# Attention on quarters of the TensorE array: state's part of y four heads at a time, scores 64 keys wide without the masked quarter

## The chip, the cores and the metric

The kernel runs on one core of a Trainium2 chip. The core has a matrix engine (TensorE, PE in the rows; its weight loads are PEld), a vector engine (VectorE, DVE), an activation engine (ScalarE, ACT), GpSimd (POOL) and a sync engine (SyncE, SP) on whose queue all DMAs of this kernel are issued. The metric is the device time of one execution in microseconds (us), as the median of several runs; lower is better.

## The reference

Three layers follow each other: a linear attention with a decaying state, a layer with `h * cos(h)`, and a gated layer. Only the first is touched by the change.

```python
def _attn_ref(q, k, v):                      # (4, 8, 768, 64): batch, heads, tokens, head size
    gamma = 1.0 - 2.0 ** (-5.0 - np.arange(H))
    scale = 1.0 / np.sqrt(D)
    for t in range(S):
        state = gamma * state + outer(k[:, :, t], v[:, :, t])
        y[:, :, t] = scale * (q[:, :, t] @ state)
    return y

def reference(...):
    x = attn_out as (3072 tokens, 512 features)
    h = x @ w_in                              # 512 x 2048
    x = (h * cos(h)) @ w_out                  # 2048 x 512
    return (silu(x @ w_gate) * (x @ w_val)) @ w2_out   # 512 x 1536, 1536 x 512
```

## The kernel before

**Attention in chunks.** Time is cut into chunks of 128 tokens (`C`) of one batch, 24 chunks in all (`NCH`; chunk `c` belongs to batch `c % 4`). A chunk has four steps. *Scores* (`scores_pe`, L306): for each of the 8 heads, a 128x128 matrix of keys against queries, in two PSUM banks `sc` (even heads in one, odd heads in the other). *Decay* (`scores_decay`, L321): DVE multiplies each bank with a table `cst` that holds the decay and zeros where the key comes after the query; the result is `s` in SBUF. *Values* (`values_pe`, L330): `y` of the chunk in one PSUM bank, first the part that comes from the state (L337, not for the first four chunks), on which the part of the chunk itself is accumulated (L344). *State* (`state_pe`, L358; `state_add`, L373): `u`, the keys against the values, is added to the state and the state is decayed, on DVE and POOL. `y` is then split into a high and a low part (`split_hi` on ACT, L113; `split_lo` on DVE, L116), which are the columns of `x` for the next layer.

The heads lie in pairs: q and k have feature rows (64 rows for the even head of a pair, 64 for the odd one), so a matmul of scores uses 64 of the 128 rows of the array, one of state's part 64 rows and 64 columns, the other matmuls of attention 128 rows and 64 columns. These matmuls are in full float32; the trace has two records for each. The large matmuls (`h` L418, `o` L501) are 128x128x512.

**The order of the work.** From the first chunks on, attention is mixed into the middle layer. This runs in 96 units: unit n makes a tile `h` (12 matmuls, L418), sends it through ACT and DVE, and PE then does the output matmuls `o` (12, L501) of the unit two before. `attn_at` (L806) lists which steps of attention stand at the end of which unit's code: chunks 4 to 7 in units 1 to 7 (with the states of 0 to 3 in unit 0), chunks 8 to 11 in units 22 to 29, and chunks 12 to 23 in units 32 to 79, four units to a chunk: scores, decay, values, state. Work for DVE and ACT that a step leaves behind (`late_mid`, `late_act`, `late_x`) runs within the next unit. In the same units ACT, DVE and POOL prepare weights (`Weight`, L121).

**Buffers.** The PSUM pool `ps_a` has two banks, tag "a": scores take both, y one, u one. `qpool` has three buffers that q and k of a chunk (`load_qk`), and k and v by token (`load_kv`), take in turn; a load waits on SP's queue until the buffer's last reader is done. `load_qk(c + 1)` stands with the scores of chunk c, `load_kv(c + 1)` with its values. Raw weights of the first layer use the places of the first eight chunks' q, k and v.

Of the kernel before, what the change touches and what calls it, by code (L numbers as in the profile page):

```python
# [20 lines left out]
DM = H * D  # L21
# [36 lines left out]
NCONST = 1548  # L58


def constants():
    gamma = 1.0 - 2.0 ** (-5.0 - np.arange(H, dtype=np.float64))
    i = np.arange(C, dtype=np.float64)
    t = np.zeros((P, NCONST), np.float64)
    head = 2 * np.arange(NP)[None, :] + (np.arange(P)[:, None] // D)
    t[:, CQ:CQ + 512] = (gamma[head][:, :, None] ** (i + 1.0) / math.sqrt(D)).reshape(P, 512)
    back = i[None, :] - i[:, None]
    by_half = gamma.reshape(NP, 2).T[None, :, :, None]
    decay = np.where(back >= 0, 1.0, 0.0)[:, None, None, :] * by_half ** np.maximum(back, 0.0)[:, None, None, :]
    t[:, CDEC:CDEC + 1024] = (decay / math.sqrt(D)).reshape(P, 1024)  # L70
    t[:, CV:CV + H] = gamma[None, :] ** -(i[:, None] + 1.0)
    t[:, CG:CG + NP] = gamma[head] ** float(C)
    return t.astype(np.float32)

# [2 lines left out]
def fused(ctx: ExitStack, tc: tile.TileContext, qkv, w1, w2, consts, out):  # L77
# [34 lines left out]
    def split_hi(src, dst):  # L112
        nc.scalar.activation(out=dst[:, 0], in_=src, func=AF.Copy)  # L113
# [156 lines left out]
    def load_qk(c, pool=qpool, tag="qkv"):  # L270
        if c >= NCH:
            return
        if pool is wpool:
            both = wpool.tile([P, 4, 512], F32, tag=tag, name="qkv")
            qkv_t[c] = [both[:, 0:2], both[:, 2:4]]
        else:
            qkv_t[c] = [pool.tile([P, 2, 512], F32, tag=tag, name="qk")]
        nc.sync.dma_start(out=qkv_t[c][0].rearrange("p a b -> p (a b)"), in_=qkv[c, :, 0:1024])

    def load_kv(c, part=slice(0, 2)):  # L280
        if c >= NCH:
            return
        if len(qkv_t[c]) == 1:
            qkv_t[c].append(qpool.tile([P, 2, 512], F32, tag="qkv", name="kv"))
# [35 lines left out]

    def scores_decay(c, half, place=None):  # L321
        if half == 0:
            p, t = place or (spool, "s")
            s_t[c] = p.tile([P, 2, 4, C], F32, tag=t, name="s")
        nc.vector.tensor_tensor(
            out=s_t[c][:, half], in0=ps_t.pop((c, half)),
            in1=cst[:, CDEC + 512 * half:CDEC + 512 * half + 512].rearrange("p (a b) -> p a b", a=4), op=ALU.mult,
        )

    def values_pe(c, place=(ps_a, "a")):  # L330
        qk, kv = qkv_t[c]
        first = c < B
        y = place[0].tile([P, NP, C], F32, tag=place[1], name="y")
        if not first:
            for h in range(H):
                r = slice(D * (h % 2), D * (h % 2) + D)
                nc.tensor.matmul(  # L337
                    out=y[r, h // 2, :], lhsT=states[c % B][r, h // 2, :],
                    rhs=qk[r, 0, (h // 2) * C:(h // 2 + 1) * C],
                    start=h < 2, stop=False, skip_group_check=True,  # L340
                )
        for h in range(H):
            r0 = D * (h % 2)
            nc.tensor.matmul(  # L344
                out=y[r0:r0 + D, h // 2, :],
                lhsT=kv[:, 1, h * D:(h + 1) * D],
                rhs=s_t[c][:, h % 2, h // 2, :],
                start=first and h < 2, stop=h >= H - 2, skip_group_check=True,
            )
        ps_t[c, "y"] = y  # L350

    def values_x(c):
        j, o = c // CPB, (c % CPB) * C
        if o == 0:
            x_t[j] = xpool.tile([P, 2, KD, T], F32R, tag=f"x{(j + (j > 1)) % 2}", name="x")
        return ps_t.pop((c, "y")), x_t[j][:, :, :, o:o + C]

    def state_pe(c, place=(ps_a, "a")):  # L358
        if c // B == NCB - 1:
# [25 lines left out]
    def attn_scores(c, place=None, load=True):  # L385
        if load:
            load_qk(c + 1)
        scores_pe(c)
        scale_queries(c)
        scale_keys(c)  # L390
        late_mid.append(lambda: scores_decay(c, 0, place))

    def attn_decay(c):
        late_mid.append(lambda: scores_decay(c, 1))

    def attn_values(c, place=(ps_a, "a"), load=True):
        values_pe(c, place)
        if load:
            load_kv(c + 1)
        y, x = values_x(c)  # L400
        late_act.append(lambda: split_hi(y, x))
        late_x.append(lambda: split_lo(y, x))
# [301 lines left out]
    def second_layer():  # L704
# [97 lines left out]
    n6 = len(units)  # L802


    o2 = (ps_o, "o2")
    attn_at = {  # L806
        0: [(attn_state, 0), (attn_state, 1), (attn_state, 2, o2), (attn_state, 3, (ps_o, "o3"))],
        1: [(attn_scores, CPB + 1, None, False), (attn_decay, CPB + 1), (attn_values, CPB, o2, False)],
        2: [(attn_values, CPB + 1, (ps_a, "a"), False)],
        3: [(attn_scores, CPB + 2, None, False), (attn_decay, CPB + 2)],  # L810
        4: [(attn_values, CPB + 2, (ps_a, "a"), False), (attn_state, CPB)],
        5: [(attn_scores, CPB + 3, None, False), (attn_decay, CPB + 3)],
        6: [(attn_values, CPB + 3, (ps_a, "a"), False), (attn_state, CPB + 1)],
        7: [(attn_state, CPB + 2), (attn_state, CPB + 3)],
    }
    for i in range(2 * CPB):
        c = 2 * CPB + i // 2
        attn_at[HEAD + M1 - 1 + i] = [(step, c) for step in four_steps[2 * (i % 2):2 * (i % 2) + 2]]
# [38 lines left out]
    with tc.manual_schedule():  # L857
        warm = tmp.tile([P, T], F32, tag="r", name="warm")
        nc.vector.memset(warm, 0.0)
        wz = warm.bitcast(mybir.dt.bfloat16)  # L860
        idle = ps_h.tile([P, T], F32, tag="h", name="idle")

# [43 lines left out]

        def first_decay(c):
            for half in range(2):
                scores_decay(c, half, (wpool, "w11") if c % 2 else None)

        def first_hi(c):
            first_x[c] = values_x(c)
            split_hi(*first_x[c])

        first_x = {}
        steps = {
            "sc": first_scores, "m": first_decay, "y": values_pe, "xh": first_hi,
            "xl": lambda c: split_lo(*first_x[c]), "k": scale_keys, "q": scale_queries,
        }
        for a in (  # L920
            "sc0 m0 y0 sc1 xh0 xl0 m1 size0 y1 xh1 xl1 low0 round0 sc2 m2 y2 merge0 xh2 sc3 m3 hi0 xl2 lo0 "
# [24 lines left out]
        for n, (kind, j, m, first, last) in enumerate(units):  # L946
            if n == n5:
                run(late_act)
                run(late_x)
                run(late_mid)  # L950
                attn.close()
                w2pool.append(ctx.enter_context(tc.tile_pool(name="w2pool", bufs=1)))
                for i in range(2):
                    Place(w2pool[0], f"v{i}").give()
                Twin("x1")
            if HEAD + 1 <= n < M1 + 1:
                fetch_w1(n - 1)
            elif n == M1 + 1:
                load_qk(2 * CPB)
                load_kv(2 * CPB)  # L960
            a, b = take(halves_at.get(n, 0)) if n < FIRST2 else take2(n)
            hidden1(j, m, first, a, b, n == 0)
            if n == FIRST2 or jobs2.get(n, "x")[0] == "b":
                fetch_w2()
            for step, *args in x_at.get(n, []):
                step(*args)
            pending.append((kind, j, m, first, last))
            steps = attn_at.get(n, [])
            if n == HEAD - 1:
                for step, *args in steps:  # L970
                    step(*args)
                steps = []
            while len(pending) > SKEW:
                output_unit(*pending.pop(0))
            for step, *args in steps:
                step(*args)
# [58 lines left out]
```

## Time and profile before

| | |
|---|---|
| median of 3 runs | 1191.59 us (1190.84 to 1195.01) |
| the profiled execution | 1192.35 us |
| its span, first to last instruction | 1190.6 us |
| PE busy | 1168.4 us, 98% of the span |
| PEld busy | 952.1 us |
| DVE, ACT, POOL busy | 644.4, 588.4, 105.4 us |
| granted clock of TensorE, mean | 0.996 of full speed |

Matmuls are pipelined and overlap in the rows, so the time that a group of matmuls costs is read from where the next group starts, not from its busy time. Attention and the middle layer fill the span up to about 648 us; after that the gated layer runs, which the change does not touch.

### The profile page before, as it was taken

Reading aid. Unit: us, or ns where it says so; the run is one execution under the profiler, and the core shown is the slowest. Engines: PE = TensorE matmul, PEld = TensorE weight load, DVE = VectorE, ACT = ScalarE, POOL = GpSimd, SP = SyncE. Lnnn points to the kernel's source line nnn. Section 1 sums busy time; section 2 is a strip of 40 time slices with the busy share of each in tenths; the row PEclk is TensorE's granted clock in tenths of the full one; section 3 lists DMA queues with packets and bytes.
Section 4 is the critical chain, followed back from the end, with each engine's and each line's share of the span. In section 5 each row is a group of like instructions: output and inputs, shape, how many; then the busy total and the mean of one; then the engine's idle time right before and its main releaser. Section 6 shows DMA issues by size and latency. Waiting matters only on the chain.

```text
span 1190.6 us, 15278 instructions
## 1 busy us (share of the span) xinstructions
PE 1168.4 (98%) x6096; PEld 952.1 (80%) x6096; DVE 644.4 (54%) x953; ACT 588.4 (49%) x847; POOL 105.4 (9%) x98
## 2 busy tenths in 40 slices
PE   7899999999999999999999999999999999999998
PEld 5688878887887878888888888878888888888877
DVE  4866764346566656666656555574444474444430
ACT  4958973346666666676855334342233342232220
POOL 2621211111211111110000000000000000000000
PEclk9999999999999999999999999999999999999999
DMA  9407833224886698588676646666448566546451
GB/s 363 194 4 276 321 125 108 97 98 181 318 323 234 232 343 320 170 310 316 250 274 240 245 160 240 246 229 248 195 164 322 208 241 266 194 157 267 169 238 36
DMA packets 54215, 265.51 MB, mean 223 GB/s; under 512 B 5760, under 2 KB 6016, under 8 KB 33152
## 3 DMA queue, kind: packets, MB, share of 16 engines
q1 hardware_dynamic: 54144, 264.53, 59.5%
q8 instruction: 48, 0.79, 0.3%
q14 instruction: 23, 0.19, 0.0%
HBM read 213.13 MB, written 51.38 MB: 222 GB/s over the span
## 4 chain that ended last, share of the span: by engine, by line
PE 89%; ACT 5%; DVE 2%; issue 2%; DMA 1%; POOL 1%; SPq 0%; DVEq 0%; POOLq 0%
PE h L418 20%; PE o L501 19%; PE o L688 16%; PE X L637 16%; PE Z L637 8%; PE Y L637 4%; ACT rw L146 2%; PE sc L314 2%; PE y L344 2%; PE y L337 2%; DMA rw<-in_w_dram 1%; PE u L365 1%; ACT f L130 1%; ACT w L113 1%; ACT g L481 0%
## 5 line engine op out<-in xcount | busy, mean ns | idle before, releaser
L688 PE MATMUL o<-wo,g 128*128 128x512 f32 x864 | 207.6, 392 | 1.4 <-ACT g L668 1.4
L418 PE MATMUL h<-x,w 128*128 128x512 f32 x780 | 193.0, 396 | 2.0 <-ACT w L113 1.7
L688 PEld LDWEIGHTS o<-wo,g 128*128 128x128 f32 x864 | 163.1, 189 | 36.4 <-ACT g L668 1.9
L501 PE MATMUL o<-g,w 128*128 128x512 f32 x780 | 187.7, 389 | 1.1 <-DVE x L116 1.1
L418 PEld LDWEIGHTS h<-x,w 128*128 128x128 f32 x780 | 144.1, 188 | 36.0 <-ACT w L113 2.5
L501 PEld LDWEIGHTS o<-g,w 128*128 128x128 f32 x780 | 146.2, 188 | 31.9 <-issue 1.5
L637 PE MATMUL X<-xo,wh 128*128 128x512 f32 x576 | 144.5, 389 | 0.0
L637 PEld LDWEIGHTS X<-xo,wh 128*128 128x128 f32 x576 | 108.0, 188 | 22.8 <-DVE xo L603 0.4
L668 ACT ACTIVATE g<-silu 128x512 fp32r<-128x512 f32 x72 | 45.5, 633 | 155.0 <-DVE silu L667 155.0
L461 ACT ACTIVATE n<-h 128x512 int32<-128x512 f32 x96 | 57.0, 594 | 92.8 <-PE h L418 92.4
L418 PE MATMUL h<-x,back 128*128 128x512 f32 x372 | 91.4, 394 | 0.0
L501 PE MATMUL o<-g,back 128*128 128x512 f32 x372 | 89.3, 389 | 0.0
L146 ACT ACTIVATE rw<-rw,above 128x1024 uint16<-128x1024 uint32 x34 | 89.0, 2618 | 0.1
L778 DVE TENSOR_TENSOR u<-Z,u 128x512 f32<-128x512 f32 x36 | 24.9, 691 | 116.5 <-PE Z L637 116.5
L501 PEld LDWEIGHTS o<-g,back 128*128 128x128 f32 x372 | 69.8, 188 | 14.5
L418 PEld LDWEIGHTS h<-x,back 128*128 128x128 f32 x372 | 68.7, 188 | 15.8 <-issue 1.2
L637 PE MATMUL Z<-xo,wh 128*128 128x512 f32 x288 | 73.2, 389 | 0.0
L637 PE MATMUL X<-x,wh 128*128 128x512 f32 x288 | 73.1, 389 | 0.0
L671 DVE TENSOR_TENSOR g<-silu,g 128x512 fp32r<-128x512 f32 x72 | 49.8, 692 | 36.0 <-ACT g L668 34.3
L131 POOL TENSOR_SCALAR f<-f 128x1024 f32<-128x1024 f32 x34 | 40.4, 1187 | 266.4 <-ACT f L130 266.3
L637 PEld LDWEIGHTS Z<-xo,wh 128*128 128x128 f32 x288 | 54.0, 188 | 11.4 <-ACT p L767 0.2
L637 PEld LDWEIGHTS X<-x,wh 128*128 128x128 f32 x288 | 54.1, 188 | 11.2
(661 smaller groups left out, 1438.8 us busy)
## 6 DMA issues: line engine op xcount, KB each, us to landing
wh<-w2d SPq DMA_DIRECT2D x36, 1024.0 KB, 7.5
wo<-w2d SPq DMA_DIRECT2D x36, 1024.0 KB, 6.5
rw<-in_w_dram SPq DMA_DIRECT2D x34, 1024.0 KB, 7.0
back<-w1d SPq DMA_DIRECT2D x31, 1024.0 KB, 6.2
wh<-w2d SPq DMA_DIRECT2D x36, 768.0 KB, 4.3
w2d<-parts SPq DMA_DIRECT2D x18, 1024.0 KB, 4.3
xo<-x2d SPq DMA_DIRECT2D x19, 512.0 KB, 7.4
w1d<-w SPq DMA_DIRECT2D x9, 1024.0 KB, 4.8
```

What stands on the lines that cost most here:

```text
L131: nc.gpsimd.tensor_scalar(out=self.f, in0=self.f, scalar1=LARGE, scalar2=SMALL, op0=ALU.min, op1=ALU.max)
L146: nc.scalar.activation(out=self.raw.bitcast(U16)[:, :, 2], in_=self.raw[:, :, 0].bitcast(U32), func=AF.Identity, scale=2.0**-29, bias=above,)
L314: nc.tensor.matmul(out=ps_t[c, half][:, i, :], lhsT=qk[r0:r0 + D, 1, p0:p0 + C], rhs=qk[r0:r0 + D, 0, p0:p0 + C], start=True, stop=True,)
L337: nc.tensor.matmul(out=y[r, h // 2, :], lhsT=states[c % B][r, h // 2, :], rhs=qk[r, 0, (h // 2) * C:(h // 2 + 1) * C], start=h < 2, stop=F ...
L418: nc.tensor.matmul(out=ps, lhsT=w[:, a, k * P:(k + 1) * P], rhs=x[:, b, k, :], start=n == 0, stop=n == len(order) - 1,)
L461: nc.scalar.activation(out=n, in_=h, func=AF.Identity, scale=TURN)
L501: nc.tensor.matmul(out=o_t[0][i], lhsT=w[:, a, i * P:(i + 1) * P], rhs=g[:, b, :], start=first and n == 0, stop=last and n == 2,)
L637: nc.tensor.matmul(out=ps, lhsT=w[:, a, k * P:(k + 1) * P], rhs=x[:, b, k, :], start=start and n == 0, stop=n == len(order) - 1, skip_grou ...
L668: nc.scalar.activation(out=g[:, 0], in_=s, func=AF.Copy)
L671: nc.vector.tensor_tensor(out=g[:, 1], in0=s, in1=g[:, 0].bitcast(F32), op=ALU.subtract)
L688: nc.tensor.matmul(out=o_t[0][i], lhsT=g[:, a, i * P:(i + 1) * P], rhs=w[:, b, :], start=m == 0 and n == 0, stop=m == M2 - 1 and n == 2,)
L778: nc.vector.tensor_tensor(out=u2, in0=Z, in1=u2, op=ALU.add)
```

## The change

Four things are done.

**Scores.** The 128 keys of a pair of heads are taken as two halves of 64. The first half is multiplied with all 128 queries, the second only with the later 64, since keys 64 to 127 against queries 0 to 63 are masked. Each matmul has 64 rows and 64 columns of the array. For every other pair the two halves of the keys change places in the partitions (`rotated`), also in the table, in k and v by token and in the key scales, so that the long and the short matmuls are spread over both column halves.

**Decay.** It multiplies only what was computed: per bank one 128x(4x64) and two 64x(2x64) instructions instead of one 128x512. The quarter that is never written stays zero: `s` is now two fixed tiles that are zeroed once at the start.

**Values.** y is in two PSUM banks, even heads in the first and odd heads in the second. The heads are arranged (`FEATURES`, `BANK`) so that the eight matmuls of state's part lie on all four quarters of the array. The features of x thereby have another order, which the rows of `w_in` follow. The split of y is done bank by bank.

**Order.** The states of 7 and 6 stand together in unit 7, those of 5 and 4 in unit 8; chunk 8 begins in unit 21; the states of 8 and 9 stand alone in units 24 and 27, those of 10 and 11 together in unit 31. From chunk 12 on the units are as before. `load_qk(c + 2)` now stands with the state of chunk c.

```diff
+FEATURES = [(0, 2), (4, 6), (3, 1), (7, 5)]
+BANK = {h: (k // 2, k % 2, half) for k, two in enumerate(FEATURES) for half, h in enumerate(two)}
+HALF = C // 2
+def rotated(a, axis_token, axis_head):
+    a = np.moveaxis(a, (axis_token, axis_head), (0, 1))
+    odd = (np.arange(H) // 2 % 2).astype(bool)
+    a = np.where(odd.reshape((1, H) + (1,) * (a.ndim - 2)), np.roll(a, HALF, 0), a)
+    return np.moveaxis(a, (0, 1), (axis_token, axis_head))
...
     def scores_pe(c, places=((ps_a, "a"), (ps_a, "a"))):
...
         for i in range(NP):
-            for half in range(2):
-                r0, p0 = D * half, C * i
-                nc.tensor.matmul(
-                    out=ps_t[c, half][:, i, :],
-                    lhsT=qk[r0:r0 + D, 1, p0:p0 + C],
-                    rhs=qk[r0:r0 + D, 0, p0:p0 + C],
-                    start=True, stop=True,
-                )
+            for part in range(2):
+                for half in range(2):
+                    r0, p0, k0 = D * half, C * i, HALF * part
+                    c0 = HALF * ((part + i) % 2)
+                    nc.tensor.matmul(
+                        out=ps_t[c, half][c0:c0 + HALF, i, k0:],
+                        lhsT=qk[r0:r0 + D, 1, p0 + k0:p0 + k0 + HALF],
+                        rhs=qk[r0:r0 + D, 0, p0 + k0:p0 + C],
+                        start=True, stop=True, skip_group_check=True,
+                    )
+    def scores_decay(c, half, place=0):
+        s_t[c] = s_all[place]
+        dec = cst[:, CDEC + 512 * half:CDEC + 512 * half + 512].rearrange("p (a b) -> p a b", a=4)
+        sc = ps_t.pop((c, half))
+        for r, pairs, i in (
+            (slice(0, P), slice(0, 4), slice(HALF, C)),
+            (slice(0, HALF), slice(0, 4, 2), slice(0, HALF)),
+            (slice(HALF, P), slice(1, 4, 2), slice(0, HALF)),
+        ):
+            nc.vector.tensor_tensor(
+                out=s_t[c][r, half, pairs, i], in0=sc[r, pairs, i], in1=dec[r, pairs, i], op=ALU.mult
+            )
...
-        y = place[0].tile([P, NP, C], F32, tag=place[1], name="y")
+        y = [p.tile([P, 2, C], F32, tag=t, name="y") for p, t in places]
         if not first:
             for h in range(H):
                 r = slice(D * (h % 2), D * (h % 2) + D)
+                bank, slot, half = BANK[h]
                 nc.tensor.matmul(
-                    out=y[r, h // 2, :], lhsT=states[c % B][r, h // 2, :],
+                    out=y[bank][D * half:D * half + D, slot, :], lhsT=states[c % B][r, h // 2, :],
...
-    def attn_state(c, place=(ps_a, "a")):
+    def attn_state(c, place=(ps_a, "a"), load=True):
         state_pe(c, place)
+        if load:
+            load_qk(c + 2)
         late_mid.append(lambda: state_add(c))
...
+        7: [(attn_state, c, (ps_a, "a"), False) for c in (7, 6)],
+        8: [(attn_state, c, (ps_a, "a"), False) for c in (5, 4)],
+        21: scores_of(8), 22: [(attn_values, 8)], 23: scores_of(9), 24: [(attn_state, 8)],
+        25: [(attn_values, 9)], 26: scores_of(10), 27: [(attn_state, 9)], 28: [(attn_values, 10)],
+        29: scores_of(11), 30: [(attn_values, 11)], 31: [(attn_state, 10), (attn_state, 11)],
...
+        s_all = [p.tile([P, 2, 4, C], F32, tag=t, name="s") for p, t in ((spool, "s"), (wpool, "w11"))]
+        for t in s_all:
+            nc.vector.memset(t, 0.0)
```

PE around the scores of chunk 8, before. `w_1455` is the weight tile of unit 22 (the last of that block), `w_974` that of unit 23.

```order
L418 MATMUL h<-x,w_1455 128x512 x12
L501 MATMUL o_936<-g,w_1330 128x512 x3
L501 MATMUL o_937<-g,w_1330 128x512 x3
L501 MATMUL o_938<-g,w_1330 128x512 x3
L501 MATMUL o_939<-g,w_1330 128x512 x3
L314 MATMUL sc<-qk 128x128 x8
L418 MATMUL h<-x,w_974 128x512 x12
```

The same place after; `w_1573` is now the weight tile of unit 22.

```order
L333 MATMUL sc<-qk 64x128 x2
L333 MATMUL sc<-qk 64x64 x2
L333 MATMUL sc<-qk 64x128 x2
L333 MATMUL sc<-qk 64x64 x2
L333 MATMUL sc<-qk 64x128 x2
L333 MATMUL sc<-qk 64x64 x2
L333 MATMUL sc<-qk 64x128 x2
L333 MATMUL sc<-qk 64x64 x2
L446 MATMUL h<-x,w_1573 128x512 x12
```

Eight matmuls have become sixteen smaller ones, and they stand ahead of the hidden tile of unit 22 instead of behind it.

SP's queue around the loads of chunk 12, before: `qk_1884`, `kv_1953` are chunk 12's, `kv_1834` chunk 11's, `qk_2073` chunk 13's.

```order
L286 DMA kv_1834<-in_qkv_dram 128x1024
L278 DMA qk_1884<-in_qkv_dram 128x1024
L286 DMA kv_1953<-in_qkv_dram 128x1024
L278 DMA qk_2073<-in_qkv_dram 128x1024
L490 DMA ev_2112<-x2d0_90 128x512
```

The same place after: `kv_2145`, `qk_2195` are chunk 12's, `kv_2025` chunk 11's, `qk_2206` chunk 13's.

```order
L301 DMA kv_2025<-in_qkv_dram 128x1024
L301 DMA kv_2145<-in_qkv_dram 128x1024
L293 DMA qk_2195<-in_qkv_dram 128x1024
L293 DMA qk_2206<-in_qkv_dram 128x1024
L518 DMA ev_2293<-x2d0_90 128x512
```

The load of chunk 12's q and k has moved behind that of its k and v by token, into the place of a buffer that the state of chunk 10 reads last.

## Rows read from the trace of the kernel before

**Rows 1.** The page: busy time (share) xinstructions, and PE's busy tenths by slice.

```profile
PE 1168.4 (98%) x6096; PEld 952.1 (80%) x6096; DVE 644.4 (54%) x953; ACT 588.4 (49%) x847; POOL 105.4 (9%) x98
PE   7899999999999999999999999999999999999998
```

**Rows 2.** PE's waits: who waited for whom, us in total, times, longest.

```profile
PE y L344 <- DVE s L325: 4.2, 8, 1.1
...
PE sc L314 <- DVE st L378: 2.3, 1, 2.3
...
PE h L418 <- ACT w L113: 1.7, 2, 0.8
...
PE o L501 <- DVE x L116: 1.1, 1, 1.1
```

**Rows 3.** Timeline of PE, chunk 0's y: start us, us, line, xrecords, [idle before].

```profile
7.66 0.43 PE L344 MATMUL y<-s,qkv 128*64 128x128 f32 x2 [0.78 <-DVE s L325]
...
8.26 1.09 PE L344 MATMUL y<-s,qkv 128*64 128x128 f32 x14 [0.16 <-DVE s L325]
```

**Rows 4.** Timeline of PE: a unit without attention, then chunk 12's values and state, chunk 13's scores.

```profile
131.31 2.88 PE L418 MATMUL h<-x,w 128*128 128x512 f32 x12
...
136.75 2.88 PE L418 MATMUL h<-x,w 128*128 128x512 f32 x12
...
255.25 1.09 PE L337 MATMUL y<-qk,st 64*64 64x128 f32 x16
256.27 1.09 PE L344 MATMUL y<-s,kv 128*64 128x128 f32 x16
257.30 3.02 PE L418 MATMUL h<-x,w 128*128 128x512 f32 x12
260.15 2.88 PE L501 MATMUL o<-g,w 128*128 128x512 f32 x12
262.96 0.69 PE L365 MATMUL u<-kv 128*64 128x64 f32 x16
263.58 3.02 PE L418 MATMUL h<-x,w 128*128 128x512 f32 x12
266.43 2.88 PE L501 MATMUL o<-g,w 128*128 128x512 f32 x12
269.24 1.16 PE L314 MATMUL sc<-qk 64*128 64x128 f32 x16
270.33 3.02 PE L418 MATMUL h<-x,w 128*128 128x512 f32 x12
```

**Rows 5.** Groups by line and form: xcount, busy us, mean ns of one, idle before.

```profile
L314 PEld LDWEIGHTS sc<-qk 64*128 64x128 f32 x256 | 15.5, 187 | 5.6 <-issue 5.3 <-DVE ev L433 0.4
...
L337 PEld LDWEIGHTS y<-qk,st 64*64 64x64 f32 x256 | 13.6, 132 | 5.6 <-issue 5.6
```

**Rows 6.** Timeline of PE: chunk 8's values and state in one unit.

```profile
179.17 1.09 PE L337 MATMUL y<-qk,st 64*64 64x128 f32 x16
...
181.68 3.02 PE L418 MATMUL h<-x,w 128*128 128x512 f32 x12
```

**Rows 7.** Timeline of PE: the hidden tile of unit 22.

```profile
166.73 3.03 PE L418 MATMUL h<-x,w 128*128 128x512 f32 x12 [0.82 <-ACT w L113]
```

**Rows 8.** The page, DMA issues: xcount, KB each, median us to landing.

```profile
rw<-in_w_dram SPq DMA_DIRECT2D x34, 1024.0 KB, 7.0
...
qk<-in_qkv_dram SPq DMA_DIRECT2D x16, 512.0 KB, 6.7
```

**Rows 9.** Timeline of DVE: the copies of four states, and chunk 12's second decay.

```profile
37.97 1.41 DVE L378 COPY st<-u 128x256 f32<-128x256 f32 x4
...
254.63 0.68 DVE L325 TENSOR_TENSOR s<-sc,cst 128x512 f32<-128x512 f32 x1
```

**Rows 10.** Timeline of ACT, unit 11.

```profile
107.02 0.60 ACT L461 ACTIVATE n<-h 128x512 int32<-128x512 f32 x1 [0.99 <-PE h L418]
```

**Rows 11.** Busy time by stretch: length; PE, PEld, DVE, ACT, POOL; clock, DMA share, GB/s.

```profile
107.00:167.00 60.00, 57.97 (x253) 47.06 (x253) 42.83 (x56) 57.35 (x65) 10.34 (x7) 1.00 0.68 252
```

More of the change, by code (lines that the diff above doesn't have):

```diff
@@ L276, in load_qk @@
         else:
-            qkv_t[c] = [pool.tile([P, 2, 512], F32, tag=tag, name="qk")]
+            qkv_t.setdefault(c, [None, None])[0] = pool.tile([P, 2, 512], F32, tag=tag, name="qk")
         nc.sync.dma_start(out=qkv_t[c][0].rearrange("p a b -> p (a b)"), in_=qkv[c, :, 0:1024])
@@ L282, in load_kv @@
             return
[L283 to L284 removed]
+        if qkv_t.setdefault(c, [None, None])[1] is None:
+            qkv_t[c][1] = qpool.tile([P, 2, 512], F32, tag="qkv", name="kv")
         n0, n1 = 512 * part.start, 512 * part.stop
@@ L336, in values_pe @@
                 r = slice(D * (h % 2), D * (h % 2) + D)
+                bank, slot, half = BANK[h]
                 nc.tensor.matmul(
-                    out=y[r, h // 2, :], lhsT=states[c % B][r, h // 2, :],
+                    out=y[bank][D * half:D * half + D, slot, :], lhsT=states[c % B][r, h // 2, :],
                     rhs=qk[r, 0, (h // 2) * C:(h // 2 + 1) * C],
-                    start=h < 2, stop=False, skip_group_check=True,
+                    start=slot == 0, stop=False, skip_group_check=True,
                 )
[L342 to L349, printed above, removed]
+        for two in FEATURES:
+            for h in two:
+                bank, slot, half = BANK[h]
+                nc.tensor.matmul(
+                    out=y[bank][D * half:D * half + D, slot, :],
+                    lhsT=kv[:, 1, h * D:(h + 1) * D],
+                    rhs=s_t[c][:, h % 2, h // 2, :],
+                    start=first and slot == 0, stop=slot == 1, skip_group_check=True,
+                )
         ps_t[c, "y"] = y
@@ L355, in values_x @@
             x_t[j] = xpool.tile([P, 2, KD, T], F32R, tag=f"x{(j + (j > 1)) % 2}", name="x")
-        return ps_t.pop((c, "y")), x_t[j][:, :, :, o:o + C]
+        y = ps_t.pop((c, "y"))
+        return [(y[n], x_t[j][:, :, 2 * n:2 * n + 2, o:o + C]) for n in range(2)]
     def state_pe(c, place=(ps_a, "a")):
@@ L383, in state_add, with attn_scores @@
         )
-    def attn_scores(c, place=None, load=True):
-        if load:
-            load_qk(c + 1)
+    def attn_scores(c):
         scores_pe(c)
@@ L802, in fused, with scores_of @@
     n6 = len(units)
-    o2 = (ps_o, "o2")
+    o2, o3, two = (ps_o, "o2"), (ps_o, "o3"), [(ps_a, "a")] * 2
+    def scores_of(c):
+        return [(attn_scores, c), (attn_decay, c)]
     attn_at = {
[L807 to L814, printed above, removed]
-    }
-    for i in range(2 * CPB):
-        c = 2 * CPB + i // 2
-        attn_at[HEAD + M1 - 1 + i] = [(step, c) for step in four_steps[2 * (i % 2):2 * (i % 2) + 2]]
+        0: [(attn_state, c, place, False) for c, place in enumerate(two + [o2, o3])],
+        1: scores_of(5) + [(attn_values, 4, (o2, o3), False)],
+        2: [(attn_values, 5, two, False)], 3: scores_of(6), 4: [(attn_values, 6, two, False)],
+        5: scores_of(7), 6: [(attn_values, 7, two, False)],
+        7: [(attn_state, c, (ps_a, "a"), False) for c in (7, 6)],
[3 more added lines that the diff above has]
+        29: scores_of(11), 30: [(attn_values, 11)], 31: [(attn_state, 10), (attn_state, 11)],
+    }
     for j in range(3, NB):
@@ L1009, in by_tile @@
         return w.reshape(r // P, P, c // P, P).transpose(2, 1, 0, 3).reshape(c // P, P, r)
+    rows = np.concatenate([np.arange(h * D, h * D + D) for two in FEATURES for h in two])
     qkv = np.concatenate([by_feature(q), by_feature(k), by_token(k), by_token(v)], axis=2)
-    w1 = np.concatenate([by_tile(words("moe_w_in")), words("moe_w_out").reshape(M1, P, DM)], axis=2)
+    w1 = np.concatenate([by_tile(words("moe_w_in")[rows]), words("moe_w_out").reshape(M1, P, DM)], axis=2)
     def by_pair(w):
```

44 lines of the change are left out of this document (23 added, 21 removed).

## The prediction

> **What bounds the kernel now.** I read the page first, then PE's waits, then the timeline of PE where attention lies. PE is busy 98% of the span, 9 tenths in nearly every slice; only the first two slices (some 30 us each) show 7 and 8 [rows 1]. The waits agree: all that matter here are short and early, y for DVE's decay (4.2 us), scores for the state copies (2.3), the outputs for x (1.1), and later two waits of hidden tiles for weights (1.7) [rows 2]. So from about 50 us on a microsecond taken from PE's stream is a microsecond of the kernel, and DVE (54%) and ACT (49%) have room, except in 107 to 167 us, where ACT is busy 57.35 of 60 us [rows 1, 11].
>
> What do the small matmuls cost? In chunk 0's y, the first head runs alone: two records take 0.43 us. The fourteen records behind them, six for even heads and eight for odd ones, take 1.09 us [rows 3]. The reader is to see that fourteen take what sixteen take elsewhere [rows 4]: each half of the columns works through its own records in turn, both at the same time, and the longer turn sets the time. Six more records in a turn cost 1.09 - 0.43 = 0.66, so a record of 128 columns costs **0.11 us in a turn**, two turns side by side. A record of 64 columns: u's group lasts 263.58 - 262.96 = 0.62, that of the chunk's own part of y 257.30 - 256.27 = 1.03 [rows 4]; eight records a turn differ by 0.41, so 0.05 less, **0.06 us**.
>
> A unit without attention takes 136.75 - 131.31 = 5.44, its h and its o 2.72 each. Entering and leaving attention costs too: around u, the outputs before take 262.96 - 260.15 = 2.81 and the hidden tile after 266.43 - 263.58 = 2.85 [rows 4]. So a state alone in its unit costs 0.62 + 0.09 + 0.13 = 0.84, and one behind a y only 0.46 (two parts of y and u last 181.68 - 179.17 = 2.51, without u 257.30 - 255.25 = 2.05) [rows 4, 6].
>
> **State's part of y.** Eight matmuls are sixteen records: before, two turns of eight. On four quarters there are four turns of four, which saves 4 x 0.11 = 0.44, less 0.01 for starting four turns instead of two: 0.43 each. It counts for chunks 5 to 23, 19 times (chunk 4's ends in an early wait, below): **-8.2 us**.
>
> **Scores.** Before, two turns of eight records of 128 columns, 0.88. After, each quarter has four records of 128 and four of 64 columns in its turn: 4 x 0.11 + 4 x 0.06 = 0.68, so 0.20 less. The first weight load of a group stands bare; with 64 columns instead of 128 it takes 132 ns instead of 187 [rows 5], 0.05 less. 0.25 to 0.27, say 0.26, for chunks 6 to 23, 18 times: **-4.7 us**.
>
> Neither row shows four quarters at once. Rows of 64 (scores, state's part) and columns of 64 (y, u) each run two at a time; that both together give four is a conclusion, and what it costs if false is the second rival.
>
> **States.** Before, six stand behind a y (0.46), one pair in unit 7 (0.84 + 0.46 = 1.30), eight alone. After, three pairs, two alone and the same eight. 3 x 1.30 + 2 x 0.84 - 6 x 0.46 - 1.30 = **+1.5 us**. This is the visible price of the new order.
>
> **Chunk 8's scores ahead of unit 22.** There PE waits 0.82 us for the weights that ACT makes [rows 7]; the scores now stand in that wait and fill it: **-0.8**, or 0 if PE is later by then and no longer waits.
>
> **Loads of chunk 12.** Its q and k now wait, behind its k and v, for the state of chunk 10, which runs in unit 31; the scores that need them come at the end of unit 32. From the end of that state to those scores PE has the state of 11 (0.46), one h and one o with their edges (2.85 + 2.81), about 6.1 to 6.2 us. The loads are 512 KB each; one alone lands in 6.7 us, a load of 1024 KB in 7.0 [rows 8]. Nearest is 7.0, since both go at once: a new stall of **+0.8**, from 0 (early enough) to 2.5 (chunk 13's load and four x loads share the engines). Behind it on SP stand only loads needed later. In unit 34 the k and v of chunk 13 wait the same way for the state of 12 in unit 35; they are wanted two units after, so nothing.
>
> **Decay and the two banks.** A 128x512 product takes 0.68, a 128x256 at most 1.41 / 4 = 0.35 [rows 9]; a 64x128 isn't shown, bounded by 0.18 (half of that) and 0.35. Per bank 0.35 + 2 x 0.18 to 0.35, 0.71 to 1.05 instead of 0.68; I take 0.8, nearer the small end, as time goes with elements here. Over 48 banks this is 1.4 to 18 us of DVE work, hidden under PE where DVE is half idle. It shows only where PE waits for the decay: y now takes both banks of the pool, the second as soon as odd heads' scores are read. Chunk 12's second decay ends at 254.63 + 0.68 = 255.31, just behind the start of its y at 255.25 [rows 4, 9]. There I expect 0.3; at the other chunks nothing. **+0.3**, from 0 to 3.6 (all twelve later chunks). The split by banks costs ACT and DVE a fixed part more per chunk, hidden likewise.
>
> **The early part.** Up to some 50 us PE waits for others [rows 2], so what the first six chunks' scores and chunk 4's y save is mostly waited away: shorter scores bring y's decay forward, a longer decay pushes it back, and y's first bank is split while the second is still computed. The two zeroings lie ahead of the first scores, with DVE idle. I take **-0.3**, from -1.5 to +1.5.
>
> **The stretch where ACT is the bound.** By then PE is 1.5 to 2 us ahead. ACT last waited for PE at unit 11, 0.99 us [rows 10], and after that hardly idles [rows 11]. Its work there is released by PE's tiles and by loads that PE's states release, so it moves along; if loads held it, up to 1.8 us would be given back.
>
> **Sum.** -8.2 - 4.7 + 1.5 - 0.8 + 0.8 + 0.3 - 0.3 = -11.4 us. The profiled execution took 1192.35 us (span 1190.6), so 1180.95; it lies 0.76 above the median of the runs, 1191.59, so I forecast a median of **1180.2 us**.
>
> **Rivals.** *Records can't follow each other that fast.* Scores now have 32 records in 0.68 us, 21 ns each on average. The densest that a row shows is u, sixteen in 0.62 less the bare part of the first load, at 0.06 for two, some 28 to 30 ns each [rows 4]. If that is an issue rate and not the array's, 32 records need about 0.90, the scores gain only the shorter first load (0.05), and 18 x 0.21 = 3.8 us are lost: 1184.0. State's part (16 x 28 ns = 0.45) would stay near its 0.44. For it: nothing denser is in the trace. Against: 0.06 is half of 0.11 as 64 columns are of 128, so u looks bound by columns. The Trainium skill's page "TensorE: Matmul & The Clock Gate", section "Wait — 56ns, not 53.3ns?", speaks against the change here: start to start never drops below about 25 ns however small the matmul. By it the scores would take an estimated 32 x 25 = 0.80 us, and the total would be some 1182.3; no row shows a denser series, so the trace leaves that open.
>
> *Four quarters don't run at once.* A quarter in the other half of the columns but the same rows waits. State's part gains nothing. Scores: per pair of heads, two records of 128 and then two of 64 in turn, 0.34, four times 1.36 instead of 0.88, less 0.05: +0.43 each, +7.7. With +1.5, -0.8, +0.8 and 0 for the rest: 1191.6 + 9.2 = **1200.8**, slower than before. It decides from the overlap: between this (+9.2) and my forecast (-11.4) lie 20.6 us, so it is even at 45% of full overlap, that is when a round of four records takes 0.17 rather than 0.11 (0.22 without overlap). Against it: both kinds of pairing run freely in the rows. For it: no row has them together.
>
> *The new waits eat the gain.* y's second bank waits for the late decay in all twelve later chunks (3.6 instead of 0.3), chunk 12's load stalls 2.5, ACT's stretch gives back 1.8: +6.8 on the forecast, 1187.0.
>
> **How the numbers follow.** Forecast 0.58 (1176.5 to 1183), record rate 0.16 (1182 to 1185.5), new waits 0.13 (1183 to 1188), no overlap 0.11 (about 1201), better than all 0.02. About 0.5% (6 us) is what a measurement of this kernel can tell from no change. Faster by more, under 1185.6: 0.58 + 0.16 + 0.02 and a little of the waits, 0.77; within 0.5%: 0.12; slower: 0.11. The range 1176.5 to 1187.5 takes in the first three.
>
> **What the next profile would show.** State's part of y, sixteen records, from 1.02 us to about 0.59 before the chunk's own part starts; scores from 270.33 - 269.24 = 1.09 to about 0.83. If scores stay near 1.05 the record rate is right; if state's part stays at 1.02 and scores grow to 1.5, quarters don't overlap. A wait of chunk 12's scores for a DMA of under 1 us; no wait at unit 22. New entries among PE's waits for DVE's decay in the later chunks, or a third slice with less than 9 tenths, would make the forecast wrong.

## The result, and the profile after

The changed kernel takes **1182.10 us** (median of 4 runs, 1180.48 to 1182.69) against 1191.71 us beside it; the ratio is 0.9912 with a 95% interval of 0.9891 to 0.9933. A second set of five runs of the same kernel gave 1181.45, ratio 0.9921 (0.9908 to 0.9935); the nine together have a median of 1181.96. The forecast was 1180.2 us, the range 1176.5 to 1187.5, faster with a chance of 0.77: the side and the range hold, and the gain is 9.6 instead of 11.4 us. The profiled execution took 1182.69 us, with a span of 1180.9.

The page of the kernel after, busy time and PE's tenths (before: [rows 1]):

```profile
PE 1156.9 (98%) x6480; PEld 938.6 (79%) x6480; DVE 659.4 (56%) x1075; ACT 591.5 (50%) x871; POOL 106.3 (9%) x98
PE   7899999999999999999999999999999999999998
```

PE is 11.5 us less busy, DVE 15.0 us more, and PE is still the bound. PE's waits after (who waited for whom, us in total, times, longest; before: [rows 2]):

```profile
PE sc L333 <- DVE st L406: 3.4, 1, 3.4
...
PE y L371 <- DVE s L350: 1.1, 2, 0.7
PE h L446 <- ACT w L128: 0.8, 1, 0.8
...
PE o L529 <- DVE ev L536: 0.7, 1, 0.7
...
PE y L363 <- DVE s L350: 0.2, 1, 0.2
```

One of the two waits of `h` for weights is gone, as forecast. New is `o` for `ev`, with a wait of state's part behind it: outputs that wait for DVE's addition of an earlier partial sum. It wasn't in the prediction. The scores' wait for the state copies in the early part has grown from 2.3 to 3.4.

The timeline of PE after, scores of chunk 13 and y of chunk 13 (before: chunk 12's y and chunk 13's scores in [rows 4]):

```profile
266.23 0.90 PE L333 MATMUL sc<-qk 64*64 64x128 f32 x32
267.06 3.01 PE L446 MATMUL h<-x,w 128*128 128x512 f32 x12
...
278.17 0.67 PE L363 MATMUL y<-qk,st 64*64 64x128 f32 x16
278.76 1.09 PE L371 MATMUL y<-s,kv 128*64 128x128 f32 x16
279.79 3.02 PE L446 MATMUL h<-x,w 128*128 128x512 f32 x12
```

State's part takes 278.76 - 278.17 = 0.59 instead of 1.02, the scores 267.06 - 266.23 = 0.83 instead of 1.09: the two numbers that the prediction gave as its test. Net of everything (from the last large matmul ahead of a group to the seventh behind it, less 7 x 0.2267, the step of the large matmuls) a y costs 1.847 instead of 2.273, a group of scores 1.053 instead of 1.320. Where PE doesn't wait, these nets are equal to 0.002 us in all groups but two (the first y of this kernel that has a state's part and no wait, 1.858, and the scores of chunk 8 at unit 22, 1.129).

The table compares where each hidden tile `h` starts with its start in the kernel before, in us (negative is earlier). It is worked out from the first L446 or L418 row of each unit; all kernels below are read this way. "Gated" is the first matmul of the gated layer, "last" its last one of the products with x. All rows are measured against one execution of the kernel before, so differences between rows say more than the rows themselves.

| kernel | unit 3 | unit 8 | 22 | 34 | 36 | 80 | gated | last | span |
|---|---|---|---|---|---|---|---|---|---|
| after | -0.20 | -2.53 | -1.24 | -4.22 | -3.01 | -10.64 | -10.64 | -10.68 | -9.70 |
| after, again | +0.15 | -2.18 | -0.82 | -3.79 | -2.61 | -10.24 | -10.24 | -11.91 | -10.99 |
| two turns | -0.70 | -2.18 | -0.89 | -2.17 | -1.33 | -4.26 | -4.26 | -4.29 | -3.34 |
| full scores | -1.17 | -2.96 | -1.46 | -3.38 | -3.69 | -8.38 | -8.38 | -8.44 | -8.42 |
| order only | -1.68 | -2.63 | -1.15 | -1.36 | -1.36 | -1.36 | -1.36 | -1.41 | -1.42 |
| loads ahead | +0.32 | -2.01 | -0.72 | -3.69 | -4.11 | -11.74 | -11.74 | -13.39 | -13.06 |
| longer decay | +4.10 | +2.72 | +3.99 | +1.01 | +2.36 | -5.27 | -5.27 | -6.91 | -6.92 |

From unit 36 to 80 the kernel after gains 7.63. Between 34 and 36 it loses 1.21, although a y lies there that should have gained 0.43: some 1.6 us are lost in one place.

### The profile page after: what moved, and what is told of

The parts are those of the page before. It is cut to its first block, busy times and chain, and to the rows that moved or that the text cites. A ratio compares the mean times of both kernels' runs of the same rounds, so it can differ in the third digit from the quotient of the medians.

```text
span 1180.9 us, 16207 instructions
## 1 busy us (share of the span) xinstructions
PE 1156.9 (98%) x6480; PEld 938.6 (79%) x6480; DVE 659.4 (56%) x1075; ACT 591.5 (50%) x871; POOL 106.3 (9%) x98
## 4 chain that ended last, share of the span: by engine, by line
PE 90%; ACT 5%; issue 2%; DVE 1%; DMA 1%; POOL 1%; SPq 0%; DVEq 0%; POOLq 0%
PE h L446 20%; PE o L529 19%; PE o L716 16%; PE X L665 16%; PE Z L665 8%; PE Y L665 4%; PE y L371 2%; ACT rw L161 1%; PE sc L333 1%; PE y L363 1%; PE u L393 1%; DMA rw<-in_w_dram 1%; ACT f L145 1%; ACT w L128 1%; ACT n L489 0%
## 5 line engine op out<-in xcount | busy, mean ns | idle before, releaser
L446 PE MATMUL h<-x,w 128*128 128x512 f32 x780 | 193.2, 397 | 1.2 <-ACT w L128 0.8
L446 PEld LDWEIGHTS h<-x,w 128*128 128x128 f32 x780 | 143.9, 189 | 34.9 <-issue 1.9
L446 PE MATMUL h<-x,back 128*128 128x512 f32 x372 | 91.3, 394 | 0.0
L446 PEld LDWEIGHTS h<-x,back 128*128 128x128 f32 x372 | 68.7, 188 | 15.5 <-issue 1.2
L665 PEld LDWEIGHTS Z<-xo,wh 128*128 128x128 f32 x288 | 54.0, 188 | 11.4 <-ACT p L795 0.2
```

Source lines behind the costliest of these rows:

```text
L446: nc.tensor.matmul(out=ps, lhsT=w[:, a, k * P:(k + 1) * P], rhs=x[:, b, k, :], start=n == 0, stop=n == len(order) - 1,)
L665: nc.tensor.matmul(out=ps, lhsT=w[:, a, k * P:(k + 1) * P], rhs=x[:, b, k, :], start=start and n == 0, stop=n == len(order) - 1, skip_grou ...
```

## The experiments

**Part by part.** First, are the gains those of the four quarters, and do the parts add up? Three kernels undo or do one part alone.

State's part on two quarters:

```diff
-FEATURES = [(0, 2), (4, 6), (3, 1), (7, 5)]
+FEATURES = [(0, 1), (2, 3), (4, 5), (6, 7)]
```

> The kernel after, with the heads arranged so that state's part of y lies on two of the four quarters (even heads on rows and columns 0 to 63, odd heads on 64 to 127), and nothing else changed. Theory (the overlap of four quarters is what gained there): state's part goes back from 0.59 to 1.02 us, 19 times, so +8.1 on 1182.1: 1190.2 us, 1189 to 1191. Rival (the gain came with the two banks or the order, and PE would have waited there anyway): 1182 to 1183 with the waits of PE moved, not taken away.

Measured: 1189.47 us (11 runs), 7.5 more than the kernel after. The net of a y is back at 2.273; the scores stay at 1.053. The theory holds; the missing 0.6 fits the lost place: there this kernel loses 0.84 between units 34 and 36, since the longer state's part hides half of the wait.

Scores and decay as before:

```diff
-            for part in range(2):
-                for half in range(2):                # sixteen matmuls, 64 keys
+            for half in range(2):                    # eight matmuls, 128 keys
...
-        for r, pairs, i in (...):                    # three products a bank
+        nc.vector.tensor_tensor(out=s_t[c][:, half], in0=sc, in1=dec, op=ALU.mult)
```

> The kernel after, with the scores and the decay of the kernel before (eight matmuls of 128 keys, one 128x512 product for each bank), state's part still on four quarters, order as after. Theory: scores go back from 0.83 to 1.09 us and cost 0.267 net more, 18 times: +4.8 on 1182.1, 1186.9 us; the shorter decay (1.3 instead of 1.9 us a chunk) gives at most 0.6 of that back, at chunk 12. Rival (the longer decay costs about what the scores gain): 1182 to 1184.

Measured: 1183.26 us (5 runs), only 1.3 more: nearer to the rival. The matmuls do what the theory says (net 1.320 again; from unit 36 to 80 it gains 4.69 where the kernel after gains 7.63, and the 2.94 between them are 11 x 0.267), but this kernel doesn't lose the 1.6 us at units 34 to 36 and is 0.4 to 0.8 earlier at unit 8. So the scores change, taken whole, was worth 1.3 us by the medians and 2.2 by the traces (-8.44 against -10.68 in "last"), not 4.8. By the traces the rest went in two places: 1.6 us at units 34 to 36 and some 1.0 up to unit 8. Why, the next kernels ask.

The new order alone, on the kernel before:

> The kernel before, with only the new order: steps of attention in the units of the kernel after, the loads of q and k with the states; scores, decay and y in one bank as before. Theory (the stall of units 32 to 34 comes from the longer decay and the two banks of y): six states out from behind a y cost 1.5, chunk 8's scores in the wait of unit 22 give 0.8 back: +0.7 on 1191.7, 1192.4 us, no wait of PE over 0.5 us in units 32 to 34. Rival (the stall comes with the order, since the fourth load of a sum stands late on SP's queue either way): 1.5 more, 1193.9 us, with a wait of o for the sum in unit 33 of about 0.7.

```diff
-        if load:
-            load_qk(c + 1)                           # with the scores
...
+        if load:
+            load_qk(c + 2)                           # with the state
...
-        4: [..., (attn_state, CPB)], 6: [..., (attn_state, CPB + 1)], 7: [(attn_state, CPB + 2), (attn_state, CPB + 3)],
+        7: [(attn_state, c, ...) for c in (7, 6)], 8: [(attn_state, c, ...) for c in (5, 4)],
+        21: scores_of(8), 22: [(attn_values, 8)], ... 31: [(attn_state, 10), (attn_state, 11)],
```

Measured: 1192.03 against 1191.50 us beside it (11 and 21 runs), ratio 1.0008 (1.0000 to 1.0017): +0.5 for an expected +0.7, and no wait of PE over 0.3 us from unit 23 to 35. The order is a small price, and the stall doesn't come with it. (That its row in the table is negative is the spread of the early part: its trace is 2.63 ahead of the one trace of before at unit 8 already.)

**The lost place.** Timeline of DVE, kernel after, units 32 to 34, then SP's queue and PE there:

```profile
244.81 1.88 DVE L536 TENSOR_TENSOR ev<-o,ev 128x512 f32<-128x512 f32 x3
250.39 0.69 DVE L536 TENSOR_TENSOR ev<-o,ev 128x512 f32<-128x512 f32 x1 [3.70 <-DMA ev<-x2d]
251.00 0.68 DVE L505 SCALAR_TENSOR_TENSOR r__2281<-r__2281,h 128x512 f32<-128x512 f32 x1
251.59 0.91 DVE L350 TENSOR_TENSOR s<-sc,cst 128x256 f32<-128x256 f32 x3
```

```profile
233.07 0.84 SPq L293 DMA_DIRECT2D qk<-in_qkv_dram  x2
233.97 1.49 SPq L518 DMA_DIRECT2D ev<-x2d  x3
245.52 0.32 SPq L541 DMA_DIRECT2D x2d<-ev  x1
245.88 0.44 SPq L518 DMA_DIRECT2D ev<-x2d  x1
```

```profile
251.14 0.96 PE L529 MATMUL o<-g,w 128*128 128x512 f32 x3 [0.72 <-DVE ev L536]
252.03 0.43 PE L363 MATMUL y<-qk,st 64*64 64x128 f32 x2
252.65 0.66 PE L363 MATMUL y<-qk,st 64*64 64x128 f32 x14 [0.19 <-DVE s L350]
```

The outputs of unit 31 add a partial sum that lies in DRAM. Three of its four loads go out at 233.97; the fourth stands on SP's queue behind the first store, at 245.88, and its add starts at 250.39. DVE works in order, so the second decay of chunk 12 stands behind that add. PE's next outputs need the bank that the add frees (0.72), and y's second bank needs the decay (0.19). In the kernel before, the same add came at 253.42 and the decay at 254.63 [rows 9], just ahead of the y: the chain was there, with no slack to spare. Timeline of DVE, kernel before:

```profile
253.42 0.69 DVE L508 TENSOR_TENSOR ev<-o,ev 128x512 f32<-128x512 f32 x1 [2.51 <-DMA ev<-x2d]
```

All four loads issued ahead:

```diff
-        part = [part_of(j, i) for i in range(2)] if again else []
+        part = [part_of(j, i) for i in range(KD)] if again else []
...
-                    if i + 2 < KD:
-                        part.append(part_of(j, i + 2))
```

> The kernel after, with all four loads of the earlier partial sum issued ahead of unit 31's outputs, where two were issued and the other two behind the first two sums. Theory (the late fourth load holds DVE's add, and the decay of chunk 12 stands behind the add on DVE): the 0.88 at the outputs of unit 31 and the 0.62 at chunk 12's y go, 1182.1 - 1.5 = 1180.6 us. Rival (the longer decay itself holds chunk 12's y): only the 0.88 goes, 1181.2 us, and the wait of y for s at chunk 12 stays at 0.2 us or over. Third: no change, when the load engines are the limit there: 1182.1 us.

Measured: 1179.69 us (4 runs), 2.3 less. DVE has the four adds in one piece:

```profile
245.35 2.48 DVE L536 TENSOR_TENSOR ev<-o,ev 128x512 f32<-128x512 f32 x4
247.74 0.68 DVE L505 SCALAR_TENSOR_TENSOR r__2281<-r__2281,h 128x512 f32<-128x512 f32 x1
248.34 0.92 DVE L350 TENSOR_TENSOR s<-sc,cst 128x256 f32<-128x256 f32 x3
```

The hidden tile of unit 36 moves from -3.01 to -4.11 with units 3 to 34 later by 0.5: both waits are gone, -0.42 between units 34 and 36 where +1.21 stood. That is 1.6; the rest of the 2.3 is spread between executions (below). Was the late load chance? The kernel after, unchanged, a second time:

> The kernel after, unchanged, for a second trace. Theory (the slow fourth load of the sum, 4.4 us from issue to landing where the others show 2.9 to 3.2, was bad luck of one execution): no wait of o for the sum over 0.3 us in unit 33, the hidden tile of unit 35 starts 3.9 to 4.6 us earlier than in the kernel before, and the median is 1180.5 to 1181.5 us. Rival (the wait belongs to this kernel): a wait of 0.6 to 0.8 us stands there again, unit 35 is 2.7 to 3.3 us earlier, and the median stays at 1182 us.

It wasn't: 1181.45 us, and from unit 34 to 36 it loses 1.18 again. PE's waits of that second trace:

```profile
PE o L529 <- DVE ev L536: 0.7, 1, 0.7
...
PE y L363 <- DVE s L350: 0.2, 1, 0.2
```

The wait belongs to the kernel. Why does the fourth load's add start 4.5 us behind its issue here (245.88 to 250.39) and 3.2 in the kernel with full scores? The load itself took 4.4 us against 3.1. The DMA records of the trace show one thing that differs: a packet of 16384 bytes of instructions, 1.52 us long, starts at 246.70, while this load is under way. Such a packet (0.96 to 1.87 us) lies between issue and landing in all six traces in which this load took 4.1 to 4.8 us (the kernel after twice, two turns, longer decay, and two kernels below: whole products early and u in y's bank) and in none of the three in which it took 2.9 to 3.2 (before, order only, full scores). So a load of instructions that falls on this place in some programs is the likely cause; no run moved it alone.

**The cover of the decay.** One product of the decay twice for each bank:

```diff
             (slice(0, P), slice(0, 4), slice(HALF, C)),
+            (slice(0, P), slice(0, 4), slice(HALF, C)),
```

> The kernel after, with the largest product of the decay done twice for each bank: 0.35 us more of DVE, 48 times, 17 us in all. Theory (hidden under PE but for chunk 12 and the first 50 us): chunk 12's y 0.35 to 0.7 later, the early part up to 1 us, so 1182.5 to 1183.8 us. Rival (y's second bank waits for the late decay in all twelve later chunks): 0.35 or more each, +4 us, 1186 us or more.

Measured: 1187.40 us (5 runs), +5.4. The theory's range is missed; in size this is nearer the rival, but not by its mechanism. The table tells the two apart: from unit 36 to 80 this kernel gains 7.63, the same as the kernel after to 0.01, so in the eleven later chunks the longer decay costs nothing at all. At chunk 12 it costs 0.14 (1.35 instead of 1.21 lost between units 34 and 36). The rest of the loss is all in the first units: at unit 8 this kernel is 5.25 behind the kernel after, 4.9 behind its second trace. Timeline of DVE, kernel after, chunk 3's decay and the merging of the second weight tile:

```profile
19.91 1.89 DVE L350 TENSOR_TENSOR s<-sc,cst 128x256 f32<-128x256 f32 x6 [1.56 <-PE sc L333]
...
27.29 1.89 DVE L169 SCALAR_TENSOR_TENSOR f<-rw,f 128x1024 int32<-128x1024 int32 x1
```

The same with the longer decay:

```profile
21.46 2.81 DVE L351 TENSOR_TENSOR s<-sc,cst 128x256 f32<-128x256 f32 x8 [1.56 <-PE sc L333]
...
29.76 1.89 DVE L169 SCALAR_TENSOR_TENSOR f<-rw,f 128x1024 int32<-128x1024 int32 x1
```

The edit put in 0.91 us a chunk (2.81 - 1.90), more than the 0.7 I had reckoned. Over the first eight chunks that is 7.3 us of DVE, and some 5 of them reach PE: early on DVE's order is the path, through decay, split and the weights that PE's first units need (the merging above is 2.5 us later). By that measure the change's own 1.90 - 1.29 = 0.61 a chunk can't have been free there. So whole products for chunks 0 to 7 alone, where every 64 keys take all 128 queries:

```diff
-                    c0 = HALF * ((part + i) % 2)
+                    c0, q0 = HALF * ((part + i) % 2), k0 if c >= 2 * CPB else 0
...
+        if c < 2 * CPB:
+            nc.vector.tensor_tensor(out=s_t[c][:, half], in0=sc, in1=dec, op=ALU.mult)
+            return
```

with `q0` in place of `k0` for the queries and the columns of `sc`.

> The kernel after, with one edit: chunks 0 to 7 alone take all 128 queries for every 64 keys and decay a bank with one 128x512 product (the zeroings stay). Theory (the longer decay of the first eight chunks costs 1 to 3 us there): 1179 to 1181 us. Rival (the first 50 us are set by loads and the clock, and executions of one program differ there by that much): 1181.5 to 1182.5 us, as the kernel after.

Measured: 1179.73 us (4 runs), 2.2 less than the kernel after, though 0.22 a chunk more goes into scores (net 1.274). That is in the theory's range; measured against the kernel before beside it, 1190.93 us here, the gain over the kernel after is 1.1 to 1.6. In that trace unit 8 starts at -3.82, 1.3 to 1.6 ahead of the two traces of the kernel after. But the rival's clock differs too: the mean granted clock in 10 to 50 us was 0.91, against 0.83 and 0.79. Where the clock is equal the lead is smaller: at 0.87 unit 8 starts at -3.16 with pieces (u in y's bank, below) and at -3.02 with whole products (the best kernel's second trace), at 0.83 at -2.53 and -2.97 (the kernel after; without zeroings, below). So whole products early gain 1 to 2 us by the medians here, and how much of it is DVE's order and how much the clock is not shown.

**A better version.** The later y uses half of its second bank. With u in the other half, the state can stand behind y again:

```diff
-        y = [p.tile([P, 2, C], F32, tag=t, name="y") for p, t in places]
+        full = [p.tile([P, 4, C], F32, tag=t, name="y") for p, t in places]
+        y = [t[:, :2] for t in full]
+        u_place[c] = full[1][:, 2:]...
...
+    def both(c):
+        return [(attn_values, c), (attn_state, c, None)]
```

> The kernel after, with u in the unused half of y's second bank, so that the state of chunks 8 to 19 stands straight behind its y again. Theory (a state alone costs 0.84 and one behind a y 0.46): eight in the later units save 0.38 each, 3.0, and of chunks 8 to 11 two alone and one pair save 3 x 0.38 = 1.1, so -4.2 on the kernel after: 1177 to 1178 us. Rival (the bank now comes free only when the state is added too, and scores of the next chunk wait for it): waits of sc for DVE, total within 1 us of the kernel after.

Measured: 1177.08 us (4 runs), -4.9 on the kernel after. From unit 36 to 80 it gains 10.28 instead of 7.63, 2.65 for seven states (0.38 each). PE's wait of `o` for the partial sum is 1.1 us here.

This edit and the loads ahead together:

> The two edits together: u in y's second bank, and all four loads of the partial sum ahead. Theory: -4.2 on the 1179.7 us that the loads ahead gave, 1175.5 us, 1174.5 to 1177. Rival (with u behind y, the loads of chunk 12 are early anyway and the loads ahead give nothing more): the same time as u in y's bank alone, 1177 to 1178 us.

Measured: 1176.72 us (4 runs), ratio 0.9872 (0.9859 to 0.9886) where u alone gave 0.9880 (0.9866 to 0.9893): inside the theory's range, but only 0.4 us under u alone, which is what the rival says. By the traces the loads do work: from unit 34 to 36 this kernel gains 0.66, and u alone loses 1.36, 2.0 apart. But in this execution unit 3 starts at +1.40, with u alone at -0.83, though the two programs are the same up to there. So 2.2 us between two executions of one early part hide a gain of that size, and the medians of four runs don't settle it.

With the whole products early as well:

> The kernel with u in y's bank and the loads ahead, and in chunks 0 to 7 alone every 64 keys take all 128 queries, so that one 128x512 product a bank does the decay: scores 0.2 us longer, the decay 1.29 instead of 1.90 us. Theory (in the first 50 us DVE's work sets the pace, since doubling a product of the decay cost there some 5 us for 0.9 us a chunk): 8 x 0.6 us of DVE less gives 0.7 (by the trace with full scores) to 3 us back, on 1176.7: 173.5 to 176 over 1000, that is 1173.5 to 1176.0. Rival (the early part is set by loads and by the clock, and the longer scores take what the decay gives): 1176.5 to 1177.5.

Measured: **1173.97 us** (5 runs), ratio 0.9853 (0.9836 to 0.9870), 2.8 less than without them (2.3 by the two ratios).

> The fastest kernel so far, unchanged (u in y's bank, loads ahead, whole products in chunks 0 to 7), beside the one above on the same chip. Theory: 1174.0 us again, 5 to 7 us under the one above (4.2 for u, 1.5 to 2 for the loads ahead). Rival (its first median was a lucky set): 1175 to 1177 us.

The same kernel again: 1174.82 us (4 runs), ratio 0.9863 (0.9849 to 0.9878), 4.9 under the kernel beside it (1179.73); between its theory and its rival; the nine runs of the two sets have a median of 1174.51. It is 17 us faster than the kernel before and 7.5 faster than the one after. The timeline of PE at chunk 12, in the first of its two traces, has neither wait nor gap, and u (L400, written into y's tile) behind y:

```profile
250.05 0.67 PE L370 MATMUL y<-qk,st 64*64 64x128 f32 x16
250.65 1.09 PE L378 MATMUL y<-s,kv 128*64 128x128 f32 x16
251.57 0.63 PE L400 MATMUL y<-kv 128*64 128x64 f32 x16
252.13 3.03 PE L453 MATMUL h<-x,w 128*128 128x512 f32 x12
```

And the same without the two zeroings at the start:

```diff
-        for t in s_all:
-            nc.vector.memset(t, 0.0)
```

> The same kernel without the two zeroings of s at the start, which the whole products of chunks 0 to 7 make needless. Theory (the zeroings lie ahead of the first scores, where DVE idles): the same time within 0.5 us. Rival (they hold the first decay): 0.5 to 1.8 us faster, and DVE's first decay starts earlier.

Measured: 1175.54 us (4 runs), 1.0 more than the nine runs with them: no gain. DVE's first decay starts at 6.26 us, with the zeroings at 6.15, so they lie in idle time as the prediction said. Why it is not the same to 0.5 us I can't show; in its profiled execution the gated layer took 1.5 us longer than in the first trace with them, of the kind described at the end.

## Why the prediction was right, and where not

| step | forecast | in the trace of after |
|---|---|---|
| state's part, 19 times | -8.2 | -8.1 (19 x 0.426) |
| scores, 18 times | -4.7 | -4.8 (18 x 0.267) |
| states | +1.5 | +1.5 (3 x 1.306 + 2 x 0.84 - 6 x 0.462 - 1.306) |
| chunk 8's scores in unit 22's wait | -0.8 | -1.0 |
| loads of chunk 12 | +0.8 | 0 |
| decay and two banks at chunk 12 | +0.3 | +1.5 |
| early part | -0.3 | +0.2 (second trace +0.6), not better known than 1 us |
| up to the last evacuation | -11.4 | -10.6 (the rows sum to -10.7) |
| behind it | 0 | +0.9 |

That the sum comes so near is in part luck: 0.8 too much for the loads and 0.2 too little gain at unit 22 stand against 1.2 too little for chunk 12 and 0.5 for the early part.

**Four quarters.** Right in mechanism and to the hundredth in size. The conclusion from two kinds of pairs to four at once was the uncertain step, and 0.59 and 0.83 settle it: without overlap state's part would have stayed at 1.02. The split of the scores' gain holds too: the kernel with whole scores on quarters has a net of 1.274, so 0.22 is the masked quarter, and the other 0.05 (1.320 - 1.274) fits the shorter bare weight load; 0.20 and 0.05 were forecast.

**The record rate** fell as a rival. 31 steps from the first to the last of the 32 records of scores take 0.83 - 0.16 (the step from the last record to `h`) = 0.67 us, 21.5 ns each by the trace, denser than any row of before. The Trainium skill's page "TensorE: Matmul & The Clock Gate", section "Wait — 56ns, not 53.3ns?", puts the least distance from start to start at about 25 ns; across four quarters the measurement is below that.

**The order** and unit 22: right. The wait of 0.82 [rows 7] is gone; the scores stand in its place. It was worth a little more than its idle time: from the start of unit 21 to that of unit 22 it is 6.56 us before and 6.57 after, where a unit without attention takes 5.44, so the wait had cost 1.12. Timeline of PE, kernel after:

```profile
161.78 2.88 PE L529 MATMUL o<-g,w 128*128 128x512 f32 x12
164.59 0.90 PE L333 MATMUL sc<-qk 64*64 64x128 f32 x32
165.49 3.02 PE L446 MATMUL h<-x,w 128*128 128x512 f32 x12
```

The stretch where ACT is the bound gave nothing back: units 10 to 18 all start 1.22 earlier.

**The loads of chunk 12** were mis-sized: they were issued at 233.07, the scores came at 239.09 without a wait. I took 7.0 us to landing from the median of 1024 KB loads [rows 8]; chunk 12's landed in 4.3 here, chunk 13's in 5.5.

**The step that failed** is "there I expect 0.3; at the other chunks nothing" for the decay and the two banks. The place, chunk 12, was right, and so was the nothing elsewhere. The size wasn't, because the argument went from the end of the second decay in the trace of before, 255.31, and a longer product. It took that start as given and didn't ask what stood ahead of it on DVE. That was the add, which follows a load that is only issued behind a store; the add holds not only the decay but PE's outputs too. The loads ahead took away 1.6 us there, so the late load and its add are shown as the cause. The longer decay is not: doubling its largest product adds only 0.14 us there.

**The early part** is the second. The sum held that the longer decay is mostly waited away. It also took 0.8 us a bank for the three pieces of the decay, where they take 0.95 (1.90 for two banks). The doubled product says some 5 of 7.3 us of DVE reach PE; the whole products early give 1 to 2 us back, in part perhaps by the clock. What was measured lies within the stated range of -1.5 to +1.5, but the sum set DVE's 54% of busy time against a stretch where DVE's order is the path.

**Behind the last evacuation** the profiled execution took 4.2 us (1176.68 to 1180.88) where the one of before took 3.3. The other kernels' traces have 3.2 to 4.2, without order; this is spread.

## What to carry to other kernels

Small matmuls are priced by the longest turn of any quarter of the array: find the columns per turn from two groups of different shape, and a re-tiling can be forecast to hundredths. What the saving brings along on another engine must be priced stretch by stretch: 0.9 us more of DVE a chunk cost nothing in eleven chunks, 0.14 us in the one where it stood behind a late load (the load itself cost 1.6), and some 5 us over eight chunks in the start, where that engine sets the pace. Ask for each wait what stands ahead of the releasing instruction on its own engine, not only how long that instruction is.

## What the hardware showed that was not expected

In the gated layer PE waits for ACT, 2.40 us at once, in every kernel. In seven of the fourteen traces the granted clock falls behind it, in seven it doesn't. Timeline of PE, kernel after, then loads ahead:

```profile
782.86 2.51 PE L665 MATMUL Z<-x,wh 128*128 128x512 f32 x6 [2.40 <-ACT p L795]
785.16 3.67 PE L716 MATMUL o<-wo,g 128*128 128x512 f32 x12
```

```profile
781.75 1.66 PE L663 MATMUL Z<-x,wh 128*128 128x512 f32 x6 [2.40 <-ACT p L793]
783.25 2.89 PE L714 MATMUL o<-wo,g 128*128 128x512 f32 x12
```

The stretch of 784 to 790 us in the two (length; PE, PEld, DVE, ACT, POOL busy; clock, DMA share, GB/s):

```profile
784.00:790.00 6.00, 6.00 (x22) 4.82 (x21) 3.52 (x5) 1.95 (x4) 0.00 (x0) 0.77 0.28 102
```

```profile
784.00:790.00 6.00, 6.00 (x28) 4.99 (x27) 3.87 (x6) 2.84 (x5) 0.00 (x0) 1.00 0.62 197
```

The granted 0.77 is a mean over a part at the lower level, 1.2 GHz, and a part at 2.4; the fall costs some 1.6 us (from "gated" to "last" in the table: -0.04 for the kernel after, -1.65 for loads ahead, against a trace of before that has the fall). It comes and goes between executions of one program: of the kernel after's two traces one has it. With the 2.2 us of the early part, where the clock in 10 to 50 us also differs between executions (0.77, 0.72, 0.96, 0.87 by ten us in the kernel after; 0.70, 0.79, 0.89, 0.77 in its second trace), this is the spread of one to two us that a median of four runs carries here.
